# A convolution band built on chip in place of a DRAM round trip, with w_in loaded over 128 partitions and the loads in another order

## The chip, the cores and the metric

One core of one Trainium2 chip. The metric is device time in microseconds (us) of one execution; a median of several executions is quoted.

## The reference, cut to what matters

```python
# x (8, 4096, 192), weight (8 heads, 7 taps), w_in (192, 2048), w_out (2048, 192)
w = exp(weight - max(weight, axis=-1)); w = w / (sum(w, axis=-1) + 1e-9)
y[b, s, h*24 + g] = sum over k of w[h, k] * x_padded[b, s + k, h*24 + g]   # 6 zero rows ahead of each sequence
h = y.reshape(32768, 192) @ w_in
out = (h * cos(h)) @ w_out
```

## The kernel before

The convolution is a matmul with a band matrix: in column m of a head the seven softmaxed taps stand at rows m+2 to m+8, one row lower for each further column. The two halves of the batch work on partitions 0 to 63 and 64 to 127, called lanes. TensorE does the convolution, an up-projection (w_in) and a down-projection (w_out); ScalarE computes the cosine as a shifted sine, VectorE the product h * cos(h), and GpSimd casts staged fp32 loads to bf16. The start, cut:

```python
taps = consts.tile([1, ROW], BF16)                    # one row of taps, zeros around them
...                                                   # softmax on one partition
row_d = d_pool.tile([1, ROW], BF16)                   # in DRAM
nc.scalar.dma_start(out=row_d, in_=taps)
for l in range(2):                                    # read back shifted by one for each partition
    nc.sync.dma_start(out=turned[lane[l]], in_=dram(row_d, row_d.offset, [[1, L], [1, H * L]]))
...
def load_w1(c, queues=(nc.sync, nc.scalar)):          # a quarter of w_in, one 64-partition half per queue
    st = staged[1, c] = staging([NCH, CW])
    for s, queue in enumerate(queues):
        queue.dma_start(out=st[lane[s]], in_=dram(moe_w_in, c * CW, [[Dff, L], [L * Dff, NCH], [1, CW]]))
def load_w2(c):                                       # half of w_out, on ScalarE's queue
    ...
cast(0, ...); cast(1, ...)                            # first x to bf16
nc.vector.tensor_copy(out=band[:, :, V:W], in_=flip(turned[:, :, 0:V]))
```

While the weights arrive, a "fill" works on what there is: convolutions, 13 up-projections and four down-projections. In the down-projection the two lanes add into two banks of PSUM, the memory that TensorE writes its sums to; when they change banks, GpSimd writes a one-element "mark" that the next down-projection waits for:

```python
def changeover(end):
    ins = nc.gpsimd.memset(mark, 0.0)                 # GpSimd works in program order
    order(ins, end)                                   # after the last matmul of this turn
    return ins
...
def later():                                          # GpSimd's jobs, in this order, during the fill
    yield from (lambda q=q: cast_w1(1, q) for q in range(NCH))
    yield cast_pair                                   # x to bf16
    yield lambda: load_w1(3)
    yield lambda: load_w2(0)
    yield lambda: load_w2(1)
    yield lambda: load_ahead(4)                       # the last x of the fill
    ...                                               # casts of w_in, two more of x
    yield from (lambda c=c, q=q: cast_w2(c, q) for c in range(2) for q in range(4))
    yield cast_pair                                   # the last x: ahead of the first mark
```

## Time and profile before

| | before |
|---|---|
| device time | 737.21 us, median of 3 (737.16 to 737.73) |
| span of the profiled execution | 738.3 us (that execution took 740.11 us, so it is a slow one of the fast state) |
| band ready, first up-projection | 16.65 us, 20.82 us |
| first mark begins, ends | 48.07 us, 48.16 us |
| from TensorE's start after the mark to the end | 738.3 - 48.21 = 690.1 us |

The prediction shows the lines and how they are read.

### The profile page before, as it was taken

To read this page: it belongs to the slowest core of one execution; us is meant where nothing else is said; L and a number is where in the kernel's file an instruction comes from. 1 tells how busy PE (TensorE), PEld (TensorE's weight loads), DVE (VectorE), ACT (ScalarE), POOL (GpSimd) and SP (SyncE) were. 2 spreads that over 40 slices of the span, in tenths; PEclk is the share of its full clock that TensorE was granted. 3 is DMA by queue.
4 is the path that set the end of the run, shared out by engine and by line. 5 is a ranking of instruction groups with operands and counts; after the bars stand their busy time and mean duration, and the time that the engine had idled before them with its cause. 6 is when DMAs were issued, how large, how long until landed. Compare 5 with 4: busy or idle time off the path is not lost.

```text
span 738.3 us, 27466 instructions
## 1 busy us (share of the span) xinstructions
PE 712.4 (96%) x12271; PEld 565.9 (77%) x12271; DVE 640.4 (87%) x590; ACT 588.8 (80%) x637; POOL 94.0 (13%) x340
## 2 busy tenths in 40 slices
PE   4589999999999999999999999999999999999997
PEld 4357777777877778888888888888877777777776
DVE  1578998989899899899899989898998999999994
ACT  2488888888888888888888888888888887787773
POOL 2431111110110110110111111111011000000000
PEclk7689999999999999999999999999999999999999
DMA  9968727265563462726463456371833211111102
GB/s 183 238 106 169 126 61 153 69 122 113 112 127 65 104 142 61 155 49 142 93 130 81 105 102 133 79 153 38 156 72 86 67 54 37 32 44 45 45 24 66
DMA packets 126283, 72.70 MB, mean 98 GB/s; under 512 B 52243, under 2 KB 124628, under 8 KB 126164
## 3 DMA queue, kind: packets, MB, share of 16 engines
q1 hardware_dynamic: 121712, 66.42, 42.7%
q10 hardware_dynamic: 4452, 4.52, 2.8%
q8 instruction: 96, 1.57, 0.9%
q14 instruction: 23, 0.19, 0.1%
HBM read 33.60 MB, written 25.17 MB: 80 GB/s over the span
## 4 chain that ended last, share of the span: by engine, by line
PE 93%; DMA 4%; issue 1%; DVE 1%; ACT 1%; POOL 1%; ACTq 0%; SPq 0%; POOLq 0%; DVEq 0%
PE h L254 48%; PE acc L254 45%; DMA xw<-in_moe_w_out_dram 2%; DMA turned<-row_d 1%; DMA row_d<-taps 1%; DVE g L361 0%; POOL w L219 0%; ACT L170 0%; POOL xb L156 0%; ACT cos L356 0%; ACT ct L309 0%; PE acc L456 0%; DVE osb L398 0%; ACTq L79 0%; ACT cT L459 0%
## 5 line engine op out<-in xcount | busy, mean ns | idle before, releaser
L361 DVE TENSOR_TENSOR g<-h,cos 128x1024 bf16<-128x1024 f32 x512 | 604.4, 1219 | 38.9 <-ACT cos L356 30.4
L356 ACT ACTIVATE cos<-h 128x1024 bf16<-128x1024 f32 x512 | 511.4, 1023 | 117.5 <-PE h L254 97.6
L254 PEld LDWEIGHTS <-g 64*128 64x128 bf16 x8192 | 374.8, 94 | 84.2 <-POOL mark L264 2.8
L254 PE MATMUL acc<-w,g 64*128 64x192 bf16 x8064 | 430.0, 243 | 1.7 <-issue 0.9
L254 PE MATMUL h<-cT,w 64*128 64x512 bf16 x3072 | 423.7, 380 | 1.7 <-DVE g L361 1.6
L254 PEld LDWEIGHTS <-w 64*128 64x128 bf16 x3072 | 179.0, 95 | 63.2 <-issue 7.8
L264 POOL MEMSET mark<- 1x1 f32 x192 | 16.9, 88 | 608.1 <-PE acc L254 599.5
L398 DVE COPY osb<-acc 128x384 f32<-128x384 f32 x63 | 35.1, 557 | 37.7 <-PE acc L254 37.7
L309 ACT CAST ct<-h 112x1024 bf16<-112x1024 f32 (+1 forms) x55 | 55.3, 1006 | 14.6 <-PE h L254 10.7
L156 POOL CAST xb<-xw 128x512 bf16<-128x512 f32 (+1 forms) x110 | 64.4, 615 | 14.9 <-DMA xw<-in_x_dram 14.0
L254 PE MATMUL h<-xb,band 64*128 64x192 bf16 (+8 forms) x912 | 38.0, 218 | 15.6 <-DVE band L237 7.8
L254 PEld LDWEIGHTS <-band 64*128 64x128 bf16 x912 | 32.8, 96 | 17.7 <-DVE band L237 8.0
L398 ACT COPY osb<-acc 128x384 f32<-128x384 f32 x63 | 29.8, 473 | 6.0 <-PE acc L254 6.0
L443 PE MATMUL h<-one 128*112 128x112 bf16 x80 | 6.6, 274 | 2.2 <-POOL one L186 2.2
L443 PEld LDWEIGHTS <-one 128*112 128x112 bf16 x80 | 6.5, 188 | 2.2 <-POOL one L186 2.2
L209 POOL CAST w<-xw 128x512 bf16<-128x512 f32 x12 | 6.9, 613 | 9.8 <-DMA xw<-in_moe_w_in_dram 9.8
L237 DVE COPY band<-turned 128x448 bf16<-128x448 bf16 x1 | 0.3, 277 | 7.6 <-DMA turned<-row_d 7.6
L254 PE MATMUL h<-w,g 64*128 64x192 bf16 x128 | 5.9, 243 | 0.3 <-POOL mark L264 0.3
L219 POOL CAST w<-xw 128x384 bf16<-128x384 f32 x8 | 3.7, 507 | 5.6 <-DMA xw<-in_moe_w_out_dram 5.6
L223 ACT ACT_TABLE_LOAD x1 | 1.3, 1283 | 3.5 <-DMA xw<-in_x_dram 3.5
L156 DVE CAST xb<-xw 128x512 bf16<-128x512 f32 (+1 forms) x2 | 1.0, 490 | 3.2 <-DMA xw<-in_x_dram 3.2
L309 DVE CAST ct<-h 112x896 bf16<-112x896 f32 x1 | 1.1, 1092 | 2.0 <-PE h L254 2.0
(28 smaller groups left out, 14.3 us busy)
## 6 DMA issues: line engine op xcount, KB each, us to landing
out_dram<-osb SPq DMA_DIRECT2D x63, 384.0 KB, 3.9
xw<-in_x_dram SPq DMA_DIRECT2D x60, 384.0 KB, 8.0
xw<-in_x_dram SPq DMA_DIRECT2D x10, 336.0 KB, 4.3
xw<-in_moe_w_in_dram ACTq DMA_DIRECT2D x5, 384.0 KB, 5.8
xw<-in_moe_w_out_dram ACTq DMA_DIRECT2D x2, 768.0 KB, 20.3
xw<-in_moe_w_in_dram SPq DMA_DIRECT2D x3, 384.0 KB
cT<-ct SPq DMA_TRANSPOSE x63, 2.9
xw<-in_x_dram ACTq DMA_DIRECT2D x2, 384.0 KB
```

The lines of the kernel that those rows point to most:

```text
L156: copies[j % len(copies)](out=xbs[p][:, s0:s1], in_=src)
L209: copy(out=w1[:, q, c * CW:(c + 1) * CW], in_=staged[1, c][:, q, :])
L219: nc.gpsimd.tensor_copy(out=w2[:, c * n:(c + 1) * n, :][:, fs, :], in_=staged[2, c][:, fs, :])
L223: nc.scalar.activation(out=warm, in_=wex[:, 0, 0:1], func=AF.Sin, bias=0.0, scale=0.0)
L237: nc.vector.tensor_copy(out=band[:, :, V:W], in_=flip(turned[:, :, 0:V]))
L254: ins = nc.tensor.matmul(out=o, lhsT=w, rhs=r, start=start, stop=stop, skip_group_check=True)
L264: ins = nc.gpsimd.memset(mark, 0.0)
L309: copy(out=ct[0:W, 0:n].rearrange("p j s c -> p s j c"), in_=ps[0:W, :, 0:n * L].rearrange("p s (j c) -> p s j c", c=L))
L356: nc.scalar.activation(out=cos, in_=hs[n], func=AF.Sin, bias=math.pi / 2.0, scale=1.0)
L361: nc.vector.tensor_tensor(out=g, in0=hs.pop(n), in1=cs.pop(n), op=ALU.mult)
L398: copy(out=osbs[k][:, 2 * bank:2 * bank + 2, :].rearrange("p a d -> p (a d)"), in_=src[:, 0:2 * D])
L443: nc.tensor.matmul(out=idle[0:W, 0, 0:W], lhsT=one, rhs=one, start=True, stop=True)
```

## The change

The intent: the band is ready at 6 us instead of 16, so that convolution can begin as soon as x lands; w_in loads over all 128 partitions; nearly all loads go through SyncE's queue in order of need; the convolutions of the fill use the two PSUM banks that the down-projection doesn't need yet, and the steps of the fill are put in another order. The diff, cut to its core:

```diff
-    wq = consts.tile([1, H, K], FP32)
+    STEP = 8
+    KB = STEP + K - 1
+    wq = consts.tile([KB, H, K], FP32)            # the softmax on 14 partitions at once
...
+    falls = ...                                   # ones where partition = j + k
+    slide = consts.tile([KB, FAR + 128], BF16)    # a diagonal, twice, 64 apart
-    row_d = d_pool.tile([1, ROW], BF16)
-    nc.scalar.dma_start(out=row_d, in_=taps)
-    for l in range(2):
-        nc.sync.dma_start(out=turned[lane[l]], in_=dram(row_d, ...))
+    nc.vector.tensor_tensor(out=prod, in0=falls..., in1=tap..., op=ALU.mult)
+    nc.vector.tensor_reduce(out=near, in_=prod, axis=AX.X, op=ALU.max)     # 8 columns of the band
+    for a in range(V // STEP):                    # moved down 8 rows at a time
+        nc.tensor.matmul(out=spread[:, :, STEP * a:STEP * (a + 1)], lhsT=slide[:, at:at + 128], rhs=near, ...)
+    nc.vector.tensor_copy(out=band[:, :, V:W], in_=spread)
...
-    for u in loads[:2]:
-        load_blocks(*u)                           # both blocks of the first x on SyncE's queue
+    load_blocks(*loads[0])
...
+    load_blocks(*loads[1], (nc.scalar, nc.scalar))      # the second block on ScalarE's
...
+    def load_w1(c, queue=nc.sync):
+        nc.sync.dma_start(out=st[:, 0:2], in_=dram(moe_w_in, c * CW, [[Dff, 128], [L * Dff, 2], cols]))
+        for s in range(2):
+            queue.dma_start(out=st[lane[s], 2], in_=dram(moe_w_in, (2 - 2 * s) * L * Dff + c * CW, [[Dff, L], cols]))
-        nc.scalar.dma_start(out=st, in_=moe_w_out[...])
+        nc.sync.dma_start(out=st, in_=moe_w_out[...])
+    load_w1(2); load_w1(3); load_w2(0); load_w2(1)      # all asked for ahead of the last x
...
-                    state["open"] = conv_first()
+                    state["open"] = conv_first(acc if count["d"] == 0 else None)
```

More of the change, by code (lines that the diff above doesn't have):

```diff
@@ L71 @@
     o_pool = ctx.enter_context(tc.tile_pool(name="o", bufs=3))
-    d_pool = ctx.enter_context(tc.tile_pool(name="dr", bufs=1, space=bass.MemoryType.DRAM))
     h_pool = ctx.enter_context(tc.tile_pool(name="hps", bufs=3, space=bass.MemoryType.PSUM))
@@ L75 @@
     ctx.enter_context(tc.manual_schedule())
-    wq = consts.tile([1, H, K], FP32)
-    nc.scalar.dma_start(out=wq, in_=dram(weight, 0, [[0, 1], [1, H * K]]))
+    STEP = 8
+    KB = STEP + K - 1
+    wq = consts.tile([KB, H, K], FP32)
+    nc.scalar.dma_start(out=wq, in_=dram(weight, 0, [[0, KB], [1, H * K]]))
     xws = {}
@@ L156, in cast @@
             copies[j % len(copies)](out=xbs[p][:, s0:s1], in_=src)
-    ROW = H * L + L
-    taps = consts.tile([1, ROW], BF16)
-    nc.gpsimd.memset(taps, 0.0)
-    one = consts.tile([128, W], BF16)
-    nc.vector.memset(one, 0.0)
-    for u in loads[:2]:
-        load_blocks(*u)
-    wmax = consts.tile([1, H], FP32)
+    unit = consts.tile([128, W], BF16)
+    nc.vector.memset(unit, 0.0)
+    nc.gpsimd.affine_select(out=unit, in_=unit, pattern=[[-1, W]], compare_op=ALU.not_equal, fill=1.0, base=0, channel_multiplier=1)
@@ new lines @@
+    falls = consts.tile([KB, STEP, K], FP32)
+    nc.vector.memset(falls, 0.0)
+    nc.gpsimd.affine_select(out=falls, in_=falls, pattern=[[-1, STEP], [-1, K]], compare_op=ALU.not_equal, fill=1.0, base=0,
+                            channel_multiplier=1)
+    FAR = V - STEP + BEFORE - K + 1
+    slide = consts.tile([KB, FAR + 128], BF16)
+    nc.vector.memset(slide, 0.0)
+    for l in range(2):
+        nc.gpsimd.affine_select(out=slide, in_=slide, pattern=[[-1, FAR + 128]], compare_op=ALU.not_equal, fill=1.0,
+                                base=FAR + l * L, channel_multiplier=1)
@@ L167, with keep_warm @@
+    acc = [o_psum.tile([128, T], FP32, name=f"acc{k}") for k in range(2)]
+    def keep_warm(n):
+        for _ in range(n):
+            nc.tensor.matmul(out=acc[0][0:W, 0:W], lhsT=unit, rhs=unit, start=True, stop=True)
+    keep_warm(30)
+    band = consts.tile([128, H, V + 128], BF16)
+    nc.vector.memset(band, 0.0)
+    load_blocks(*loads[0])
+    wmax = consts.tile([KB, H], FP32)
     nc.vector.tensor_reduce(out=wmax, in_=wq, axis=AX.X, op=ALU.max)
-    nc.vector.tensor_tensor(out=wq, in0=wq, in1=wmax.unsqueeze(2).to_broadcast([1, H, K]), op=ALU.subtract)
@@ L169 @@
-    wex = consts.tile([1, H, K], FP32)
+    nc.vector.tensor_tensor(out=wq, in0=wq, in1=wmax.unsqueeze(2).to_broadcast([KB, H, K]), op=ALU.subtract)
+    wex = consts.tile([KB, H, K], FP32)
     nc.scalar.activation(out=wex, in_=wq, func=AF.Exp)
-    wsum = consts.tile([1, H], FP32)
+    load_blocks(*loads[1], (nc.scalar, nc.scalar))
+    wsum = consts.tile([KB, H], FP32)
     nc.vector.tensor_reduce(out=wsum, in_=wex, axis=AX.X, op=ALU.add)
     nc.vector.tensor_scalar(out=wsum, in0=wsum, scalar1=1e-9, scalar2=None, op0=ALU.add)
-    winv = consts.tile([1, H], FP32)
+    winv = consts.tile([KB, H], FP32)
@@ L175 @@
     nc.vector.reciprocal(winv, wsum)
-    tap = taps[:, 0:H * L].rearrange("p (h j) -> p h j", h=H)
-    FIRST = V - 1 + BEFORE - K + 1
-    nc.vector.tensor_tensor(out=tap[:, :, FIRST:FIRST + K], in0=wex, in1=winv.unsqueeze(2).to_broadcast([1, H, K]), op=ALU.mult)
-    row_d = d_pool.tile([1, ROW], BF16)
-    turned = consts.tile([128, H, L], BF16)
-    band = consts.tile([128, H, V + 128], BF16)
-    nc.vector.memset(band, 0.0)
-    nc.gpsimd.affine_select(out=one, in_=one, pattern=[[-1, W]], compare_op=ALU.not_equal, fill=1.0, base=0, channel_multiplier=1)
@@ L187 @@
-    nc.scalar.dma_start(out=row_d, in_=taps)
-    for l in range(2):
-        nc.sync.dma_start(out=turned[lane[l]], in_=dram(row_d, row_d.offset, [[1, L], [1, H * L]]))
-    def flip(ap):
-        a, b, (st, n) = ap.ap
-        return bass.AP(tensor=ap.tensor, offset=ap.offset + (n - 1) * st, ap=[a, b, [-st, n]])
+    tap = consts.tile([KB, H, K], FP32)
+    nc.vector.tensor_tensor(out=tap, in0=wex, in1=winv.unsqueeze(2).to_broadcast([KB, H, K]), op=ALU.mult)
+    prod = consts.tile([KB, H, STEP, K], FP32)
@@ new lines @@
+    nc.vector.tensor_tensor(out=prod, in0=falls.unsqueeze(1).to_broadcast([KB, H, STEP, K]),
+                            in1=tap.unsqueeze(2).to_broadcast([KB, H, STEP, K]), op=ALU.mult)
+    near = consts.tile([KB, H, STEP], BF16)
+    nc.vector.tensor_reduce(out=near, in_=prod, axis=AX.X, op=ALU.max)
+    spread = acc[1][:, 0:H * V].rearrange("p (h m) -> p h m", h=H)
+    for a in range(V // STEP):
+        at = FAR - (BEFORE - K + 1) - STEP * a
+        nc.tensor.matmul(out=spread[:, :, STEP * a:STEP * (a + 1)], lhsT=slide[:, at:at + 128], rhs=near, start=True, stop=True)
@@ L197 @@
+    nc.vector.tensor_copy(out=band[:, :, V:W], in_=spread)
+    keep_warm(16)
     w1 = consts.tile([128, NCH, Dff], BF16)
@@ L201 @@
     staged = {}
-    def load_w1(c, queues=(nc.sync, nc.scalar)):
+    def load_w1(c, queue=nc.sync):
         st = staged[1, c] = staging([NCH, CW])
-        for s, queue in enumerate(queues):
-            queue.dma_start(out=st[lane[s]], in_=dram(moe_w_in, c * CW, [[Dff, L], [L * Dff, NCH], [1, CW]]))
+        cols = [1, CW]
+        nc.sync.dma_start(out=st[:, 0:2], in_=dram(moe_w_in, c * CW, [[Dff, 128], [L * Dff, 2], cols]))
+        for s in range(2):
+            queue.dma_start(out=st[lane[s], 2], in_=dram(moe_w_in, (2 - 2 * s) * L * Dff + c * CW, [[Dff, L], cols]))
     def cast_w1(c, q, copy=nc.gpsimd.tensor_copy):
@@ L213, in load_w2 @@
         st = staged[2, c] = staging([n, D])
-        nc.scalar.dma_start(out=st, in_=moe_w_out[c * n * 128:(c + 1) * n * 128, :].rearrange("(n p) d -> p n d", p=128))
+        nc.sync.dma_start(out=st, in_=moe_w_out[c * n * 128:(c + 1) * n * 128, :].rearrange("(n p) d -> p n d", p=128))
     def cast_w2(c, q):
@@ L219, in cast_w2 @@
         nc.gpsimd.tensor_copy(out=w2[:, c * n:(c + 1) * n, :][:, fs, :], in_=staged[2, c][:, fs, :])
-    load_w1(0, (nc.scalar, nc.scalar))
+    load_w1(0, nc.scalar)
     warm = consts.tile([1, 1], FP32)
-    nc.scalar.activation(out=warm, in_=wex[:, 0, 0:1], func=AF.Sin, bias=0.0, scale=0.0)
+    nc.scalar.activation(out=warm, in_=wex[0:1, 0, 0:1], func=AF.Sin, bias=0.0, scale=0.0)
     load_w1(1)
@@ L232, in load_ahead @@
             state["loaded"] += 1
-    load_ahead(1, (nc.sync, nc.scalar))
+    load_ahead(1)
     cast(0, (nc.vector.tensor_copy, nc.gpsimd.tensor_copy))
     cast(1, (nc.vector.tensor_copy, nc.gpsimd.tensor_copy))
-    nc.vector.tensor_copy(out=band[:, :, V:W], in_=flip(turned[:, :, 0:V]))
+    load_w1(2)
+    load_w1(3)
+    load_w2(0)
+    load_w2(1)
+    cast_w1(0, 0)
+    cast_w1(0, 1)
+    cast_w1(0, 2)
     def order(later, earlier):
@@ L266, in changeover @@
         return ins
-    acc = [o_psum.tile([128, T], FP32, name=f"acc{k}") for k in range(2)]
     cT = {}
@@ L276, in cast_pair, with conv_mms @@
             state["cast"] += 1
-    def conv_mms(p, ps, l):
+    def conv_mms(p, bank, l):
         slots, xb, mms = pairs[p], xbs[p], []
@@ L286, in conv_mms @@
             assert js == list(range(j0, j1))
-            out = ps[:, l, :].rearrange("p (j c) -> p j c", c=L)[:, j0:j1]
+            out = bank.rearrange("p (j c) -> p j c", c=L)[:, j0:j1]
             for h in range(H):
@@ L293, in conv_mms, with conv_first @@
         return [(*mm, j == 0, j == len(mms) - 1) for j, mm in enumerate(mms)]
-    def conv_first():
+    def conv_first(ps=None):
         p = state["conv"]
         state["conv"] += 1
-        ps = h_pool.tile([128, 2, T], FP32, name="h")
-        mms = [conv_mms(p, ps, l) for l in range(2)]
+        if ps is None:
+            ps = h_pool.tile([128, 2, T], FP32, name="h")
+        mms = [conv_mms(p, bank, l) for l, bank in enumerate(ps if type(ps) is list else (ps[:, 0, :], ps[:, 1, :]))]
         half = len(mms[0]) // 2
@@ L308, in evacuate @@
         ct = ct_pool.tile([128, 8, 2, L], BF16, name="ct")
-        copy(out=ct[0:W, 0:n].rearrange("p j s c -> p s j c"),
-             in_=ps[0:W, :, 0:n * L].rearrange("p s (j c) -> p s j c", c=L))
+        if type(ps) is list:
+            for s, bank in enumerate(ps):
+                copy(out=ct[0:W, 0:n, s, :], in_=bank[0:W, 0:n * L].rearrange("p (j c) -> p j c", c=L))
+        else:
+            copy(out=ct[0:W, 0:n].rearrange("p j s c -> p s j c"),
+                 in_=ps[0:W, :, 0:n * L].rearrange("p s (j c) -> p s j c", c=L))
         return ct
@@ L349, in up @@
         fc, tk = slice(f * 128, (f + 1) * 128), slice(t0, t0 + T)
-        lanes(*[[(h[:, l, :], w1[lane[l], c, fc], cT[b][lane[l], c, tk], T, c == 0, c == NCH - 1)
+        lanes(*[[(h[:, l, :], w1[lane[l], (c - l) % NCH, fc], cT[b][lane[l], c, tk], T, c == 0, c == NCH - 1)
                  for c in range(NCH)] for l in range(2)])
@@ L438, in emit @@
                     {"U": up, "S": sin, "M": mult}[op](n)
-    idle = h_pool.tile([128, 2, T], FP32, name="h")
-    for _ in range(80):
-        nc.tensor.matmul(out=idle[0:W, 0, 0:W], lhsT=one, rhs=one, start=True, stop=True)
     firsts = []
@@ L455 @@
             to, at = (by_chunk[3], c) if k == 4 else (by_chunk[c], k)
-            nc.tensor.matmul(out=to[:, at * W:(at + 1) * W], lhsT=ct[0:W, j].rearrange("p s c -> p (s c)"), rhs=one[0:W, :],
+            nc.tensor.matmul(out=to[:, at * W:(at + 1) * W], lhsT=ct[0:W, j].rearrange("p s c -> p (s c)"), rhs=unit[0:W, :],
                              start=True, stop=True)
@@ L460 @@
     nc.scalar.copy(cT[0][:, :, 4 * W:5 * W], by_chunk[3][:, 0:NCH * W].rearrange("p (c t) -> p c t", c=NCH))
-    load_w1(2)
-    cast_w1(0, 0)
-    cast_w1(0, 1)
-    cast_w1(0, 2)
     def later():
@@ L470, in later @@
         yield cast_pair
-        yield lambda: load_w1(3)
-        yield lambda: load_w2(0)
-        yield lambda: load_w2(1)
         yield lambda: load_ahead(4)
@@ L489, in fill @@
             emit(part)
-    fill("kkkkUSMkUSMkUSMkkkkUSMkUSMCcUSMekkCcUSMekkkUSMCcUSMekkkkkkkkUSMUSMUSMkU")
+    fill("kkkkkUSMUSMUSMkkkUSMUSMkkkUSMCceUSMkkUSMCceUSMkkkkkkkkUSMCceUSMUSMkU")
     for k in range(NSETS - 2):
```

## The prediction

> **What bounds the kernel now.** I read the busy table, then the chain of waits in its first 80 us, then GpSimd in order of time, then the stretches with granted clock and DMA rate.
>
> ```profile
> PE 712.4 (96%) x12271; PEld 565.9 (77%) x12271; DVE 640.4 (87%) x590; ACT 588.8 (80%) x637; POOL 94.0 (13%) x340
> ```
>
> TensorE idles for 738.3 - 712.4 = 25.9 us in all. A change to the start can win part of those, plus TensorE work done at half clock, and no more. The chain (start us, length us, what) tells which start-up waits count:
>
> ```profile
> 3.85 4.02 DMA row_d<-taps
> 8.48 7.76 DMA turned<-row_d
> 16.36 0.29 DVE band L237
> 20.82 2.76 PE h L254 x12
> 23.67 16.43 DMA xw<-in_moe_w_out_dram
> 40.15 1.86 POOL w L219 x4
> 45.60 1.41 POOL w L219 x3
> 47.01 1.11 POOL xb L156 x2
> 48.12 0.04 POOL mark L264
> 48.21 0.51 PE acc L254 x8
> ```
>
> The round trip of the taps through DRAM (11.8 us and the wait between) holds the band until 16.65 us. But at 23.67 us the chain leaves TensorE and follows a transfer of w_out, then GpSimd's casts, to the first mark, the tiny memset that lets the down-projection change lanes. From there TensorE runs with 0.2 us of idle per 15 us. So the time is: moment of the first mark, 48.2 us, plus fixed work. GpSimd runs in program order, so all this stands before the mark:
>
> ```profile
> 29.19 0.61 POOL L156 CAST xb<-xw 128x512 bf16<-128x512 f32 x1 [8.25 <-DMA xw<-in_x_dram]
> 45.15 1.86 POOL L219 CAST w<-xw 128x384 bf16<-128x384 f32 x4 [3.14 <-DMA xw<-in_moe_w_out_dram]
> 46.95 1.17 POOL L156 CAST xb<-xw 128x512 bf16<-128x512 f32 x2
> 48.07 0.09 POOL L264 MEMSET mark<- 1x1 f32 x1
> ```
>
> What feeds it (the last three columns are granted clock, mean busy share of the DMA engines, GB/s):
>
> ```profile
> 20.00:24.00 4.00, 3.85 (x23) 1.95 (x23) 1.55 (x3) 2.19 (x4) 0.61 (x1) 0.50 1.12 198
> 26.00:28.00 2.00, 0.75 (x6) 0.25 (x6) 1.04 (x1) 0.22 (x1) 0.00 (x0) 1.00 1.12 325
> 36.00:41.00 5.00, 3.65 (x30) 1.45 (x27) 2.06 (x2) 3.28 (x4) 2.52 (x5) 0.79 1.12 260
> 47.00:49.00 2.00, 1.81 (x30) 0.98 (x26) 1.72 (x2) 1.17 (x2) 1.15 (x4) 1.00 0.00 0
> 60.00:65.00 5.00, 4.80 (x88) 3.43 (x84) 4.66 (x5) 4.43 (x6) 0.09 (x1) 1.00 1.12 203
> ```
>
> The DMA engines are full (share 1.1) from 3 us to about 41 us, carry transposes until 46.7 us, then stop. The start is bound by bytes and their order, not by the band.
>
> **What the Trainium skill says.** "SBUF — State Buffer", section "Door 1: The DMA port swizzle", says that 64 partitions reach only 8 of 16 ports and only a transfer over 128 reaches all. The trace agrees loosely: x, always 64 partitions, moves at 203 GB/s, and 260 with w_out (128 partitions) in the mix; yet 325 GB/s occurs with 64-partition transfers alone, probably both halves at once in 2 KB rows. "DMA: Bandwidth & Descriptors", section "Queues, rings and completion order", says that each DMA engine alternates between queues per packet. The trace fits: an x half on ScalarE's queue, issued by 16.9 us and sharing with 2 KB packets, is there only at 29.19. "TensorE: Matmul & The Clock Gate", section "Part 1: The HAM clock gate", says the clock is judged over free-running windows of 3.4 us, halved after an idle one and restored after a busy one. In 1-us stretches of this trace the clock changes at about 31.3, 38.1, 41.5 and 44.9 us, spaced by 3.4 or twice that.
>
> **The change part by part.**
>
> (1) The band. Removed: both DRAM transfers. Added: a product and a reduction of 448 elements over 14 partitions, 7 small matmuls, a PSUM copy. The softmax ends at 3.82 us as now. A 56-element VectorE operation takes 0.20 us; at about 1 ns an element the two new ones take an estimated 0.6 each, to 5.1. Seven matmuls: 0.6 us at the 83 ns a warm-up matmul takes (6.65 us for 80), to 5.7; 30 warm-ups end at 2.2 + 2.5 = 4.7 and don't delay them. The copy: 0.6, as the 128x448 cT copies. Band ready at 6.4. But the first casts of x end at 8.85 (data lands at 7.4 and 8.2), so convolution starts at 8.9 instead of 16.7. The next 4.1 us (convolution, evacuation, turning, copies) keep their length: first up-projection at 12.8 instead of 20.8. This 8 us is not yet a gain.
>
> (2) The order of transfers. Nearly all are now on SyncE's queue, in this order: first x (0.97 MB), w_in chunks 0 and 1, next x (1.57), chunks 2 and 3, w_out (1.57), next x (1.57). In the program w_out comes ahead of the last x instead of beside it, and the build's instruction order shows the last x still needed by the two xb casts just ahead of the first mark. So the mark needs all 8.83 MB; only the 0.13 MB of turned is gone.
>
> (3) w_in over 128 partitions: 2.10 of 3.15 MB move in 128-partition transfers. I take 330 GB/s for those (estimate from the 325 above), 215 for the other 1.05 MB (9 to 12 us: 211), 300 for w_out alone (estimate: 260 was a mix with x), 200 for x.
>
> Landing times, in us: the first x and a part of chunk 0 as now at 8.2, the rest of chunk 0 by 10.1, chunk 1 at 12.9 (0.524/0.330 + 0.262/0.215 = 2.8), x at 20.8 (7.9), chunks 2 and 3 at 23.6 and 26.4, w_out at 29.0 and 31.6, last x at 39.5. Then one cast of 0.6: mark at about 40.2, 7.9 us earlier than 48.16.
>
> (4) Compute ahead of the mark. 13 up-projections in both, at 1.22 us each on VectorE. The seventh and later wait for the convolution after x lands (21.5), two more convolutions near 27 to 30, the last product about 34.5. The first four down-projections and one up-projection end near 34. The idle PSUM banks for the fill convolutions spare h buffers here; TensorE waits for the mark anyway, so they gain nothing by themselves.
>
> (5) The cost of waiting. TensorE then idles some 6 us, more than a clock window, and starts the steady part at half clock. It needs the rest of one window and a whole one, 3.4 to 6.8 us, mean 5.1, losing half: 2.6 us. Before, it had full clock at 48.2.
>
> Steady state and tail are the same instructions. Sum: -7.9 + 2.6 = -5.3, hence 737.2 - 5.3 = 731.9.
>
> **The rivals.** (a) The whole 8 us of the band comes through, with the w_in gain on top, and no cold start: 726 to 729. For it: the chain does begin with that round trip. Against: the chain's 16.43 us on w_out, and full DMA engines. (b) The bytes don't move faster: chunks over 128 partitions run at the old 200 to 210 GB/s. That adds 2.10/0.205 - 2.10/0.330 = 3.9 us, the mark comes at 44, and with the cold start the time is 735 to 736. For it: the engines' busy share was already 1.1, and packets stay at 2 KB. (c) The mark is early but the transposes, queued behind the last x, hold the up-projection that needs columns past 512. They took most of 41 to 46.7 us before. From 39.5 they would end near 44 to 45, while that up-projection comes about 4 us of work after the mark (near 46 when cold). It is close; a loss of up to 2 us would give 733 to 734. (d) One queue in place of two starves, since issues wait for the transfer eight before. I find always over 1 MB outstanding, and SyncE alone kept 203 GB/s at 60 to 65 us. If it did starve, 735 to 740.
>
> **Range and chances.** Extremes of the mark are 38 and 44.5, of the cold start 0 and 3.4. They don't add at their ends often, so 728.5 to 735.5. Faster by over 2% would need under 722.8 us, a mark before 34 us; 8.83 MB from 2 us on would then have to run at 276 GB/s on average, where x alone (4.1 MB) needs 20 us at its rate: 0.03. Slower by 2% would need a new wait in the steady part, which isn't touched: 0.01. Within 2%: 0.96.
>
> **What would show it.** Right: band written near 6.4 us and first convolution near 8.9; VectorE's first product near 15 instead of 23.4; over 300 GB/s while w_in moves; w_out cast well ahead of the last x; GpSimd waiting for x just before the first mark, near 40; clock 0.5 for some us after it. Wrong: a first mark after 45, a mark that waits for w_out, TensorE waiting for cT transposes after the mark, or idle time in the steady part that was not there before.

## The result, and the profile after

After: 734.75 us, median of 4 (733.1 to 735.0); before, on the same chip: 737.37 us. The ratio is 0.9959, 95% interval 0.9942 to 0.9976: a gain of 0.4%, inside "within 2%". A ratio here and below is the mean time of one kernel's fast runs over that of the other's of the same rounds, so not quite the ratio of the medians that are quoted.

The busy table of the changed kernel: TensorE now idles for 733.2 - 710.3 = 22.9 us instead of 25.9.

```profile
PE 710.3 (97%) x12244; PEld 526.8 (72%) x12244; DVE 642.1 (88%) x594; ACT 588.7 (80%) x640; POOL 94.9 (13%) x342
```

TensorE in order of time (start us, us, engine, source line, operation, tiles; in brackets the idle time ahead of it and what ended that):

```profile
7.98 1.04 PE L282 MATMUL h<-xb,band 64*128 64x96 bf16 x28
15.39 1.09 PE L282 MATMUL h<-xb,band 64*128 64x24 bf16 x40 [6.37 <-DVE xb L157]
...
18.66 5.94 PE L282 MATMUL h<-cT,w 64*128 64x512 bf16 x30 [0.15 <-POOL w L231]
...
42.55 0.82 PE L282 MATMUL acc<-w,g 64*128 64x192 bf16 x8 [5.69 <-POOL mark L292]
43.17 1.49 PE L282 MATMUL h<-cT,w 64*128 64x512 bf16 x6
```

The first convolution starts at 7.98, but only half of it: the other half waits 6.37 us more for a cast of x, and the first up-projection comes at 18.66, only 2.2 us earlier than before. Later TensorE stands 5.69 us at the mark and then needs 1.49 us for six matmuls that take 0.81 at full clock (it starts "cold"). The chain of waits (start, length, what) says what it stood for:

```profile
4.70 10.78 DMA xw<-in_moe_w_in_dram
...
17.55 9.18 DMA xw<-in_moe_w_in_dram
...
31.74 9.99 DMA xw<-in_x_dram
...
41.85 0.62 POOL xb L157
42.47 0.04 POOL mark L292
...
42.55 0.82 PE acc L282 x8
```

Three transfers carry nearly all of it; the last is x. GpSimd shows the same from its side:

```profile
35.53 1.87 POOL L241 CAST w<-xw 128x384 bf16<-128x384 f32 x4 [1.97 <-DMA xw<-in_moe_w_out_dram]
38.75 0.62 POOL L157 CAST xb<-xw 128x512 bf16<-128x512 f32 x1 [1.35 <-DMA xw<-in_x_dram]
41.85 0.62 POOL L157 CAST xb<-xw 128x512 bf16<-128x512 f32 x1 [2.48 <-DMA xw<-in_x_dram]
42.41 0.09 POOL L292 MEMSET mark<- 1x1 f32 x1
```

w_out is cast by 37.4, and x comes last, as planned. In stretches of 1 us (busy time of PE, PEld, DVE, ACT, POOL, then granted clock, the share of full speed that TensorE was given, mean busy share of the DMA engines, GB/s) the end of that transfer is not a full stream. (A share above 1 means that the packet times which the view adds up overlap; the 2.93 falls where, by packet sizes, the transposes begin.)

```profile
38.00:39.00 1.00, 0.00 (x0) 0.00 (x0) 1.00 (x1) 0.00 (x0) 0.25 (x1) 1.00 2.93 184
39.00:40.00 1.00, 0.00 (x0) 0.00 (x0) 0.18 (x1) 0.00 (x0) 0.37 (x1) 1.00 0.67 109
40.00:41.00 1.00, 0.00 (x0) 0.00 (x0) 0.00 (x0) 0.00 (x0) 0.00 (x0) 0.62 0.56 61
```

From 39 us on the engines are only 0.67 and 0.56 busy while GpSimd waits until 41.73 for the last x, and the clock falls to 0.5 within TensorE's idle stretch.

### The profile page after: what moved, and what is told of

It reads as the page before. It is cut to its first block, busy times and chain, and to the rows that moved or that the text cites. A ratio compares the mean times of both kernels' runs of the same rounds, so it can differ in the third digit from the quotient of the medians.

```text
span 733.2 us, 27421 instructions
## 1 busy us (share of the span) xinstructions
PE 710.3 (97%) x12244; PEld 526.8 (72%) x12244; DVE 642.1 (88%) x594; ACT 588.7 (80%) x640; POOL 94.9 (13%) x342
## 4 chain that ended last, share of the span: by engine, by line
PE 93%; DMA 4%; POOL 1%; DVE 0%; SPq 0%; ACT 0%; issue 0%; ACTq 0%; POOLq 0%
PE h L282 48%; PE acc L282 45%; DMA xw<-in_moe_w_in_dram 3%; DMA xw<-in_x_dram 1%; POOL xb L157 0%; POOL w L231 0%; DMA wq<-in_weight_dram 0%; DVE g L392 0%; ACTq L110 0%; ACT cos L387 0%; SPq L110 0%; SPq L228 0%; SPq L226 0%; DVE osb L429 0%; ACT osb L429 0%
## 5 line engine op out<-in xcount | busy, mean ns | idle before, releaser
L282 PEld LDWEIGHTS <-g 64*128 64x128 bf16 x8192 | 353.3, 94 | 109.5 <-POOL mark L292 9.3
L282 PE MATMUL acc<-w,g 64*128 64x192 bf16 x8064 | 415.8, 243 | 6.0 <-POOL mark L292 6.0
L282 PE MATMUL h<-cT,w 64*128 64x512 bf16 x3072 | 409.9, 379 | 2.7 <-DVE g L392 2.4
L282 PEld LDWEIGHTS <-w 64*128 64x128 bf16 x3072 | 148.2, 95 | 81.0 <-issue 7.2
L340 ACT CAST ct<-h 112x1024 bf16<-112x1024 f32 (+1 forms) x52 | 52.3, 1006 | 4.8 <-PE h L282 1.0
L282 PE MATMUL h<-xb,band 64*128 64x192 bf16 (+9 forms) x872 | 34.0, 216 | 6.4 <-DVE xb L157 6.4
L282 PEld LDWEIGHTS <-band 64*128 64x128 bf16 x912 | 30.8, 96 | 8.0 <-issue 7.3
L179 PE MATMUL acc<-unit 128*112 128x112 bf16 x46 | 4.8, 302 | 1.3 <-POOL unit L162 1.3
L179 PEld LDWEIGHTS <-unit 128*112 128x112 bf16 x46 | 4.4, 211 | 1.4 <-POOL unit L162 1.3
L338 ACT CAST ct<-acc 112x512 bf16<-112x512 f32 x6 | 3.3, 630 | 0.0
```

Source lines behind the costliest of these rows:

```text
L179: nc.tensor.matmul(out=acc[0][0:W, 0:W], lhsT=unit, rhs=unit, start=True, stop=True)
L282: ins = nc.tensor.matmul(out=o, lhsT=w, rhs=r, start=start, stop=stop, skip_group_check=True)
L338: copy(out=ct[0:W, 0:n, s, :], in_=bank[0:W, 0:n * L].rearrange("p (j c) -> p j c", c=L))
L340: copy(out=ct[0:W, 0:n].rearrange("p j s c -> p s j c"), in_=ps[0:W, :, 0:n * L].rearrange("p s (j c) -> p s j c", c=L))
```

## The experiments

Twelve runs were made, two of them of unchanged kernels. All but one gave the reference's result. "Mark" is the start of the first mark in the run's one trace, and "wait" how long TensorE stood idle there: near 0, TensorE came to the mark no earlier than the mark was set, so its own work in the fill was as late as the mark.

| kernel | what it is | median us | ratio to before (95%) | mark us | wait us |
|---|---|---|---|---|---|
| before_again | before, one look | 738.07 | one run | 46.48 | 0.1 |
| after_again | changed kernel | 733.91 | 0.9942 (0.9928 to 0.9956) | 42.26 | 5.75 |
| band_only | before + band on chip | 734.16 | 0.9953 (0.9934 to 0.9973) | 42.84 | 0 |
| all_but_band | changed, with the old band | 741.02 | 1.0035 (1.0022 to 1.0048) | 47.24 | 6.33 |
| trip_unused | band_only, trip made, not used | 733.13 | 0.9924 (0.9911 to 0.9937) | 44.84 | 0 |
| late_band | band_only, band written late | 735.15 | 0.9972 (0.9957 to 0.9987) | 44.63 | 1.49 |
| w_in_halves | changed, w_in by 64 partitions | 734.07 | 0.9944 (0.9932 to 0.9956) | 41.92 | 2.90 |
| cast_later | changed, last x cast after the mark | 733.77 | 0.9940 (0.9921 to 0.9959) | 38.52 | 1.61 |
| stay_warm | changed, TensorE kept busy | 731.45 (wrong result) | 0.9918 (0.9898 to 0.9938) | 40.23 | 0.36, after the added matmuls |
| hold_transposes | changed, transposes held back | 738.30 | 1.0030 (1.0010 to 1.0049) | 46.11 | 7.09 |
| best | a rearranged version | 727.58 | 0.9871 (0.9852 to 0.9891) | 32.99 | 0 |
| best_2 | the same, one step further | 726.82 | 0.9851 (0.9830 to 0.9871) | 34.76 | 0 |

The medians of the kernel before were 738.07, 737.96, 737.14 and 737.16 us in the four jobs, so ratios are compared, not medians. The theory at the start was the prediction's: the mark waits for bytes, and the band only moves work that waits anyway. The rival: the band itself is the gain.

### How far two executions of one kernel differ: before_again, after_again

> The kernel before, unchanged, for a second trace: the one read for the prediction came from an execution of 740.1 us, while the timed ones took 737.2 to 737.7. If start-up is bound by bytes, the first mark comes again within 1 us of 48.2 us and only the clock windows fall differently; span 735 to 738. If the start-up itself varies by microseconds from execution to execution, the mark moves by over 1.5 us.

> The changed kernel unchanged, as the yardstick for this job and for a second trace. First mark 40 to 42.5 us, half clock for some 4 us after it, ratio to before 0.994 to 0.998. If its ratio lies at 0.995 like the one of band_only (0.9953), all other parts of the change together are worth nothing on top of the band.

Before, looked at again, marks at 46.48 us, 1.6 us earlier than in the first trace, with an execution 2 us shorter: that 48.07 belonged to one slow execution. The changed kernel gives 42.26 and 42.41. So one trace places a mark to about 2 us, and differences of less than that need the timed ratios.

### Which part gives the gain: band_only, all_but_band

```diff
# band_only, against before: the band as in the changed kernel; loads, queues, w_in and fill as before
-    nc.scalar.dma_start(out=row_d, in_=taps)   # and the two reads of it
+    ... prod, near, seven matmuls, one copy
# all_but_band, against the changed kernel: the band by the old round trip, all else kept
```

> The kernel before with the band built on chip and nothing else changed. My theory: the band is off the path that sets the end, so convolution starts near 9 us instead of 16.7 but the first mark stays within 1 us of 48.2, and the time is within 1.5 us of before (ratio 0.998 to 1.002). Rival, the round trip was on the path: 7 to 8 us faster, ratio near 0.990.

> The changed kernel with the old band by the DRAM round trip, all else (128 partitions, order, fill on idle banks) kept. If the band alone made the gain, this is at the time of before (ratio 0.999 to 1.002, mark 46 to 48). If the other parts reach the same byte bound by another way, ratio 0.995 to 0.997 and mark 41 to 44. My first theory, the band off the path, expects the latter.

The band alone gives 0.9953, as much as the whole change (0.9942 and 0.9959). GpSimd's last casts in band_only:

```profile
39.92 1.86 POOL L238 CAST w<-xw 128x384 bf16<-128x384 f32 x4 [3.32 <-DMA xw<-in_moe_w_out_dram]
...
42.84 0.09 POOL L282 MEMSET mark<- 1x1 f32 x1
```

Its mark is no earlier than the changed kernel's, but TensorE was busy up to it and did not go cold. So the two equal gains end at different waits: the changed kernel waits 5.7 us for the mark, band_only for its own work in the fill. The rest without the band loses 0.35%. There the round trip stands in SyncE's queue, which by now carries nearly all loads, and the DMA engines run dry behind it (1-us stretches of all_but_band):

```profile
8.00:9.00 1.00, 0.00 (x0) 0.00 (x0) 0.27 (x1) 0.00 (x0) 0.24 (x1) 1.00 0.10 31
9.00:10.00 1.00, 0.00 (x0) 0.00 (x0) 0.62 (x2) 0.00 (x0) 1.00 (x2) 1.00 0.44 99
```

So the prediction's view that the 8 us of the band are "not yet a gain" fell: without the new band there is no gain. But it isn't the early band as such that pays. In all_but_band the first up-projection comes at 15.13 us, earlier than in band_only (16.89) and in both traces of the changed kernel (18.66 and 15.73), and still its mark is the latest of the three: its last x is cast only at 46.68.

### Round trip or lateness: trip_unused, late_band

```diff
# trip_unused, against band_only
+    nc.scalar.dma_start(out=row_d, in_=taps)   # and the two reads, into a buffer nobody uses
# late_band, against band_only
-    nc.vector.tensor_copy(out=band[:, :, V:W], in_=spread)
     cast(1, (nc.vector.tensor_copy, nc.gpsimd.tensor_copy))
+    for _ in range(7):
+        nc.vector.tensor_copy(out=band[:, :, V:W], in_=spread)
```

(The one copy removed and seven made behind the casts; the expectation below says eight in all, which counts one too many.)

> band_only with the round trip through DRAM still made at its old place in the queues, its result used by nothing. Theory A, the trip costs by what it does to the queues (SyncE stands for 3 us until the taps are in DRAM, the two halves of w_in no longer move side by side): convolution starts near 9 us, yet the mark comes at 46 to 48 as in before and the ratio is 0.999 to 1.001. Theory B, it costs by the late convolution, behind whose evacuation ScalarE issues w_in chunks 2 and 3 and w_out: mark near 43 and ratio 0.995 as in band_only.

> The kernel before with the band built on chip and no round trip at all, but the copy that writes the band is done eight times over, seven of them behind the first casts of x, so that the band is ready near 16.5 us as in the kernel before (16.65). It is the fourth cell of two questions: is there a round trip, and is the band late. Theory A (only the lateness of the band costs: the convolution's evacuation on ScalarE comes late, so ScalarE issues its next w_in half late and the DMA engines run with one half in flight from 16 to 20 us): time back at 737 to 738.5, first up-projection after 19 us, the last w_out cast waiting for its DMA past 42 us, first mark at 46 or later. Theory B (the round trip's own packets or its place in the queues cost): as band_only, 733 to 734.5, mark near 43.

The trip alone costs nothing (0.9924). That left lateness, with a clear forecast of 737 to 738.5 for a late band; late_band gave 735.15, between the two theories. Its convolution starts at 17.21 and its first up-projection at 21.33, as late as in the kernel before, and yet it keeps more than half of the gain. Theory A's one half in flight from 16 to 20 us isn't there either (below). Neither theory holds alone. Against band_only the late band may cost 1.4 us, but the two intervals overlap. trip_unused isn't a clean counterpart either: ScalarE was still issuing loads until 15.5 us, and its first up-projection came at 18.50.

The moment when the last half of w_out can be cast goes with the time, but not alone: 45.15 and 43.56 us in the two traces of before, 41.71 in late_band, 39.99 in trip_unused, 39.92 in band_only. The last two are level, and yet TensorE goes past the mark at 43.04 in band_only and at 45.25 in trip_unused. TensorE's own work in the fill is a second path. First TensorE's start after the mark in before and in band_only, then the mark of trip_unused:

```profile
48.21 0.51 PE L254 MATMUL acc<-w,g 64*128 64x192 bf16 x8 [0.19 <-POOL mark L264]
43.04 0.51 PE L272 MATMUL acc<-w,g 64*128 64x192 bf16 x8
44.84 0.09 POOL L293 MEMSET mark<- 1x1 f32 x1 [1.87 <-PE acc L283]
```

In before TensorE waits only 0.19 us; in band_only it doesn't wait; in trip_unused the mark waits 1.87 us for TensorE. The chain of waits in band_only runs through the second load of x and TensorE's fill, and not through w_out. The last half of that x is cast at 29.19 and 27.86 us in the two traces of before, 26.96 in trip_unused, 25.84 in band_only and 24.86 in late_band, where the mark is what TensorE waits for (1.49 us). So in before two paths end within 0.2 us of each other, and a change gains only what it takes from both.

The stretch in which the kernels part is 16 to 20 us. First before, then band_only (columns as above):

```profile
16.00:20.00 4.00, 3.04 (x79) 2.56 (x80) 1.60 (x3) 1.20 (x2) 1.73 (x3) 0.50 1.12 189
```

```profile
16.00:20.00 4.00, 3.69 (x23) 1.76 (x22) 1.40 (x3) 2.19 (x4) 1.43 (x3) 1.00 1.07 311
```

before_again moves 193 GB/s there, late_band 290. The trace's packet records show, as I read them, that before had only SyncE's queue in motion from 16 to 20 us (no packet of ScalarE's moved, though a block of x had been issued there by 16.86), one 64-partition half at a time, while in band_only and late_band both queues moved. That fits these four traces, but not trip_unused: it moves 219 GB/s there and makes up for it later. So it is shown that the on-chip band brings both landings forward, the second x's and w_out's, and that the later of the two paths sets the time. By which steps the round trip and the late band together hold the landings back is only partly known. The times of issue give a hint: SyncE, which waits for the taps in DRAM, issues its first half of w_in at 9.25 us in before and 9.40 in trip_unused, but at 4.76 in late_band and 4.88 in band_only; ScalarE, which comes to its half of the third chunk only behind its copies of the first convolution, issues it at 20.34 in before and 20.85 in late_band, but at 17.86 in trip_unused and 16.25 in band_only. So late_band takes away the first of these delays, and trip_unused most of the second. One more step can be read from the semaphores in the traces: in before eight of them go round over both queues, and a transfer is issued only when the earlier one with the same semaphore has landed. There the second x's last block to be issued on ScalarE's queue shares one with the round trip's second read, which lands at 16.24; that block is issued at 16.26 (14.28 in before_again, 14.90 in trip_unused), against 13.29 in band_only and 13.96 in late_band. That is one way in which the round trip holds the second x back; whether it is the largest was not tested.

### Is w_in over 128 partitions faster: w_in_halves

```diff
-        nc.sync.dma_start(out=st[:, 0:2], in_=dram(moe_w_in, c * CW, [[Dff, 128], [L * Dff, 2], cols]))
+        for s in range(2):
+            (nc.sync, queue)[s].dma_start(out=st[lane[s]], in_=dram(moe_w_in, c * CW, [[Dff, L], [L * Dff, NCH], cols]))
```

> The changed kernel with w_in loaded in halves of 64 partitions again (one half on each queue for chunk 0, both on SyncE after it). My prediction priced the 128 partitions at 3.9 us of transfer time: the mark comes 3 to 4 us later than in after_again and the time is 3 to 4 us longer. Rival, what counts is 2 KB rows over both halves of the array within a short time, however they are cut: mark and time within 1 us of after_again.

734.07 us against 733.91 in the same job: worth nothing that can be measured. The rates say how. From 24 to 28 us w_in_halves moved 227 GB/s and the two traces of the changed kernel 269 and 257; from 32 to 36 us it was the other way round:

```profile
24.00:28.00 4.00, 1.91 (x24) 1.10 (x24) 2.57 (x3) 3.15 (x5) 1.29 (x3) 1.00 1.06 227
...
32.00:36.00 4.00, 4.00 (x30) 2.10 (x28) 2.45 (x2) 3.37 (x6) 2.57 (x6) 0.51 1.12 255
```

against 217 and 222. (Part of the first difference is w_out, which by packet sizes is under way there in the changed kernel, and hardly in w_in_halves.) What was ahead while w_in moved was level again when the last x landed: the mark comes at 41.92 and 42.26.

### The wait and the cold clock: cast_later, stay_warm

```diff
# cast_later: GpSimd casts the last x in the first set of the steady part instead of ahead of the mark
-        yield cast_pair
+        yield lambda: None
# stay_warm: 60 matmuls into unused columns of an accumulator bank, ahead of the first mark
+            nc.tensor.matmul(out=acc[0][0:W, 2 * D:2 * D + W], lhsT=unit, rhs=unit, start=True, stop=True, ...)
```

> The changed kernel with the two casts of the last x moved behind the first mark in GpSimd's order; all transfers as they are. My theory, the mark waits for the last x only through GpSimd's program order: first mark at 37.4 to 38 (w_out cast at 37.4) instead of 42.5, no half clock after it; then the up-projection that needs transposed columns waits until the transposes land near 44, so the gain over the changed kernel is 3 to 5 us, 730 to 732. Rival, the mark is held by something else that ends at 42: no change, 734.7.

> The changed kernel with 60 warm-up matmuls (into unused columns of a bank) between the last up-projection and the wait for the first mark. My theory, the cold start after the mark costs half of the 4.5 us at clock 0.5: granted clock stays 1.0 through the mark at 42.5 and the time falls by 2.2 us, to 732.5. Rival, the cold stretch is made up for later by slack in the steady part: no change (within 0.5 us).

cast_later has its mark at 38.52, 3.7 us earlier and with full clock, and gains next to nothing (0.9940, where 3 to 5 us over the changed kernel were expected). TensorE is stopped by the next late thing, the transposes that stand behind the last x in SyncE's queue:

```profile
43.36 0.39 PE L282 MATMUL h<-cT,w 64*128 64x512 bf16 x2 [1.57 <-DMA cT<-ct]
45.63 1.21 PE L282 MATMUL h<-cT,w 64*128 64x512 bf16 x4 [1.88 <-DMA cT<-ct]
```

After these waits the clock is at 0.5 from 46 to 48 us, so the cold start comes all the same.

stay_warm gave a wrong result, relative error 0.0443, which was not intended. The Trainium skill, "PSUM — Partial Sum Buffer", section "The four PSUM rules", says that a matmul with the start flag clears the accumulate state of the whole PSUM bank, not only of the columns it writes. By that the four down-projections already in bank 0 were lost: a quarter of the terms in one of 128 bank fillings, and the root of 1/128 * 1/4 is 0.0442. The measured error agrees. The number and size of the instructions are those of a right kernel, so its time can be used. TensorE starts at 40.38 at full clock and needs 728.8 - 40.38 = 688.4 us to the end; the changed kernel needs 690.7 and, looked at again, 691.0. That puts the cold start at 2.3 to 2.6 us. But kernels that passed the mark at full clock needed 688.0 (trip_unused) to 690.1 us (before) from there, so the rest isn't fixed to better than 1 us, and neither is this cost. (The mark was also 2 us earlier in this trace; the matmuls can't have done that, and one trace places a mark no better.)

### Do the transposes hold up the last x: hold_transposes

```diff
-            nc.sync.dma_start_transpose(out=dst, in_=...)
+            held.append(...)                    # issued on SyncE only after the last x has been cast
```

> The changed kernel, with the transposes of the fill issued only after the last x has been cast. Theory A (transposes running beside the last transfer of x hold up its landing by 2 to 3 us): last x cast near 39.5 instead of 41.7 and the first mark near 40 instead of 42.3; the time need not fall, as the transposes then come after the mark and TensorE waits for them: 732 to 735. Theory B (x is simply that late, the transposes run in gaps): last x cast and mark stay within 0.7 us of 41.8 and 42.3, time 734 to 737.

Theory A fell: the last x is cast at 45.55, not at 39.5, and the kernel is 0.3% slower than before. (The profiled execution, 742.0 us, was the slowest of six. Its last half of w_out was cast at 39.40 instead of 35.53, so its loads were late before any held transpose could matter, and for the size of the effect the run says little.) What it does show is the end of a transfer with no transpose in flight:

```profile
41.00:42.00 1.00, 0.00 (x0) 0.00 (x0) 0.48 (x1) 0.00 (x0) 0.26 (x1) 1.00 1.08 190
42.00:43.00 1.00, 0.00 (x0) 0.00 (x0) 0.00 (x0) 0.00 (x0) 0.04 (x1) 0.87 0.57 111
43.00:44.00 1.00, 0.00 (x0) 0.00 (x0) 0.00 (x0) 0.00 (x0) 0.58 (x1) 0.50 0.41 104
44.00:45.00 1.00, 0.00 (x0) 0.00 (x0) 0.00 (x0) 0.00 (x0) 0.00 (x0) 0.50 0.17 38
```

The busy share falls to 0.57, 0.41 and 0.17 over 3 us, as it would if some engines are done while others still have a part of x; the cast waits until 45.5. The Trainium skill, "DMA: Bandwidth & Descriptors", section "Why a DMA increments its semaphore by 16 and not by 1", says that the up to 16 engines of a transfer finish independently and the semaphore counts them all; these lines, a mean over the engines, agree but don't show single engines. So in these two traces the last transfer has a tail of 2 to 3 us, with transposes beside it or not. Whether transposes lengthen it stays open.

### A version that beats both: best, best_2

```diff
# best, against the changed kernel
-    load_blocks(*loads[1], (nc.scalar, nc.scalar))
+    load_blocks(*loads[1])                      # ahead of the weights, on SyncE's queue
-        yield lambda: load_ahead(4)
-        yield cast_pair
+        yield lambda: load_ahead(2)             # the last x is asked for behind the fill's transposes
# its cast and its convolution go into the first set of the steady part
# best_2, against best: that cast behind the third mark, that convolution in the second set
-    keep_warm(16)
+    keep_warm(46)
```

> The changed kernel with the second x back on SyncE's queue ahead of the w_in chunks, the last loads of x put behind the transposes of the fill, and the last cast of x moved into the first set of the steady part, so that the mark needs only w_out. Theory A (the mark waits for bytes and for the order in which they are asked for): first up-projection near 13 us, first mark near 37.5, no idle window long enough to halve the clock after it, no wait for a transpose: 726 to 730. Theory B (the fixed work takes back what the mark gains: transposes or the late x make TensorE wait after the mark, or the clock is halved anyway): mark early but the time 731 to 735.

> The best version so far, in whose trace the third mark still waits behind a cast of x (x landed at 41.83 us, the mark came at 42.46, TensorE stood idle 2.49 us and then ran at half clock until about 46), with that cast moved behind the third mark, the next convolution moved from the end of the first set into the second set, and 30 more warm-up matmuls ahead of the first convolution, because the clock was halved from 8 to 19 us. Theory A (the late x and the cold clock after it are still on the path): no idle stretch of TensorE over 1 us between 33 and 48 us, full clock there, 723.5 to 726, some 2.5 to 3.5 us under the best version so far (727.58). Theory B (the moved convolution makes a later up-projection wait for its columns, or GpSimd's order holds another mark): a new idle stretch between 45 and 65 us and a time of 727 or more. The extra warm-ups alone should move the first products by less than 1 us and the time by nothing, as the first part waits for transfers.

best gave 727.58 us, inside theory A. The mark needs w_out only and comes at 32.99 (even earlier than expected; it waits 0.88 us for TensorE, so here both paths are short), and the first block of x, no longer beside weights, brings the first up-projection to 13.88:

```profile
13.88 4.96 PE L282 MATMUL h<-cT,w 64*128 64x512 bf16 x24 [0.15 <-ACT cT L488]
...
42.61 1.46 PE L282 MATMUL acc<-w,g 64*128 64x192 bf16 x16 [2.49 <-POOL mark L292]
```

The second line is what was left: the third mark stood behind a cast of the late x in GpSimd's order, and the clock was halved again. In best_2 that wait is gone (no idle time of TensorE over 0.25 us between 33 and 52 us, clock 1.0 throughout), as expected. Its median of 726.82 lies under best's but above the 723.5 to 726 expected, and the two intervals overlap: that step of 2.5 to 3.5 us came out at about 1 us, unproven. Which of best's edits pays how much was not tested. Its profiled execution, 725.28 us, was the fastest of five, so the trace is from the good end.

## Why the prediction was right or wrong

The predicted time was 731.9 us, in a range of 728.5 to 735.5; 734.75 was measured. The class and the range held. The shape also held: the mark waits for the last x through GpSimd's order, TensorE idles there and starts cold. But several terms were off, and one of them in kind. And "the time is: moment of the first mark plus fixed work" had a second path beside it in the kernel before: TensorE's own fill ended 0.19 us ahead of the mark, so an earlier mark alone would have gained next to nothing.

1. **The band.** "Band ready at 6.4": 7.04. "Convolution starts at 8.9": 7.98. "First up-projection at 12.8": 18.66 and, in after_again, 15.73. The late convolution comes from part 2, "first x (0.97 MB)" first in SyncE's order: the diff moves the second block of x to ScalarE's queue, beside w_in's 2 KB packets, and there it lands only at 14.78. VectorE's first product came at 21.21, not near 15. best undoes that and gets 13.88. "This 8 us is not yet a gain" was wrong: band_only, with no other part of the change, gains as much as the whole, and all_but_band nothing. The step that failed is to take the landing of the loads as independent of the band: in band_only w_out came 3.6 to 5.2 us earlier (39.92 from 43.56 and 45.15) and the second x 2.0 to 3.4 us (25.84 from 27.86 and 29.19). Neither the late band nor the round trip alone explains it, as the four cells show.

2. **The order of transfers.** Right: w_out ahead of x, x last, mark 0.7 us after x.

3. **w_in over 128 partitions, -3.9 us.** Measured at 0 by w_in_halves. That is the outcome of rival (b), whose time of 735 to 736 was nearer than the predicted 731.9, but not its mechanism: w_in didn't move at the old 200 to 210 GB/s. It moved at 257 and 269 in the stretches above, not at 330, and the lead was not kept. The 325 GB/s behind that 330 were a poor measure: by packet sizes nearly all packets from 26 to 27 us were 768-byte rows of x, on both queues, and none were of w_in on 128 partitions. The other reading of queues in the prediction doesn't hold either: of the x half on ScalarE's queue not one packet moved from 16 to 23 us, so taking turns packet by packet isn't what held it then. Why it stood is open.

4. **The fill's spare banks, 0.** Not tested by itself. The rest of the change, the new order of the fill and the spare banks together, did shorten TensorE's path: from the second convolution of the fill to the first down-projections 6.1 us (28.64 to 34.71) against 10.4 in band_only (30.63 to 41.07). In the changed kernel the late mark hides that; in best, where the mark is early, it can count.

5. **The cold start, +2.6 us.** Right in kind, and in size as far as it is known: 2.3 to 2.6 from stay_warm, known to about 1 us. The clock was at half for 4.5 us after the mark (42.55 to about 47).

The sum was -7.9 + 2.6 from a mark at 40.2. The mark began at 42.41, so its term was -5.7 against the first trace (48.07). The missing 2.2 us are the landing of the last x, 41.73 instead of 39.5. In bytes the working was on schedule: in the packet records, as I read them, as many bytes as all loads ahead of the last x hold (7.26 MB) had moved by 31.9 us, where it had 31.6, and 8.71 of the 8.83 MB by 39.0. What it left out is that here a transfer landed well after most of its bytes: w_out's last half could be cast only at 35.5, when 8.01 MB had moved, so x was already moving behind it, and the last packets of x came at 41.0. With that the sum is -5.7 + 2.5 = -3.2, or 734.0 us. That this meets 734.75 so well is partly luck: the trace of before was a slow execution, and against before_again's mark of 46.48 the mark's term is only -4.1.

Rival (a)'s time of 726 to 729 is what a better order reached: best_2 lies 1.5% under the kernel before. That is no proof of its mechanism, since best and best_2 also move loads and casts. Rival (c), transposes behind the last x, was hidden by the late mark in the changed kernel and showed as soon as cast_later removed that. Rival (d), one queue that starves, didn't happen with the new band; with the old one (all_but_band) it did.

## What to carry to other kernels

When the start of a kernel waits for loads, list the transfers in the order in which the engines need them and ask of each wait what else stands behind it in the same queue and the same engine's program order: here a cast of x that nobody needed yet held the mark, and moving it and its load behind other work, together with the first x ahead of the weights, was worth more than the change itself. Taking away only one of several late things gains little, because the next is close behind (0.2 us in the kernel before), so look how long the engine at the end of the chain really waited, and move the late things together. Don't judge an early step by whether its wait lies on the chain at the end: test it alone, as it may decide when later transfers are issued.

## What the Trainium skill lacked or had wrong

- "SBUF — State Buffer", section "Can I just issue two DMAs to hit both halves?", says that two transfers on the two halves serialize and gain 6%. Here, by my reading of which halves were moving, one half at a time gave 189 to 193 GB/s from 16 to 20 us (before, twice), and both halves from two queues gave 290 and 311 (late_band, band_only).
- The same page's advice to use 128 partitions, in "The DMA setup-cost knee", fits the rate while w_in moves (257 and 269 against 227 GB/s from 24 to 28 us, in part w_out) but brought no time: 733.91 against 734.07 us.
- "DMA: Bandwidth & Descriptors" says that the engines of one transfer finish independently; it gives no size for the spread when many transfers are queued. Here the last x trickled in for some 3 us at 111, 104 and 38 GB/s (hold_transposes).
